# Second network's first product by Strassen's seven products instead of eight

## The chip, the cores and the metric

One Trainium2 chip, one core, one launch. The metric is the device time of that core in microseconds (us), the median over runs. TensorE (PE) multiplies, ScalarE (ACT) and VectorE (DVE) do the elementwise work, GpSimd (POOL) is nearly unused, and every DMA is issued from SyncE's queue (SP).

## The reference

Softmax-normalised linear attention (4 batches, 8 heads, 576 positions, width 64) gives x of 2304 tokens by 512. Two networks follow, each with a first product 512 to 2048, an elementwise function and a second product 2048 to 512:

```python
x = _moe_ref(x=x, **moe_kwargs)        # h = x @ w_in; g = h * sigmoid(1.702 h); g @ w_out
return _moe2_ref(x=x, **moe2_kwargs)   # h = x @ w_in; g = h * tanh(softplus(h)); g @ w_out
```

The weights arrive as float64, and the kernel decodes them to float32 on the chip.

## The kernel before, in words

Tokens go in 6 blocks of NB = 384, the 2048 hidden features in 16 chunks of 128. Every float32 operand of the two networks is kept as a high and a low part (`F32R`), and each product is the sum of three matmuls: high by high, high by low, low by high (`SPLIT`).

**First network.** Step n of 96 is block n // 16, chunk n % 16. `gemm_in` (line 771) makes 4 x 3 matmuls of 384 columns into one of two PSUM banks h0, h1; `gelu` is a tanh on ACT (L784) and a product on DVE (L789); `gelu_split` copies the high part (ACT L339 or DVE) and subtracts for the low part (DVE L331); `gemm_out` of step n - 2 (L812) makes 4 x 3 matmuls into banks acc0 to acc3. The attention of the next block is mixed into these steps, on banks at0 and at1. At a block's end `x2_evac` reads acc twice, once on ACT (L837) and once on DVE (L844), and writes x2 as high and low part; four of the six blocks go to the DRAM tile `x2d` (384 KB per piece).

**Second network.** It runs over 48 pairs of chunks (6 blocks x 8 pairs). `gemm_in2` calls `gemm_in` for two chunks: 24 matmuls of 384 columns into a pair of banks hp. `mish` is one ACT operation over 768 elements (L920), a high copy and a low subtraction (L339, L331). `gemm_out2` of pair n - 2 makes 18 matmuls of 512 columns (L945) that accumulate over the 8 pairs into three of the four acc banks. `out_evac` (L965, L966) copies them out after the eighth pair. All weights of the second network are decoded once by `weight` and then stay in SBUF in the tiles W0 to W15; a chunk's w_in part is split into high and low there like everything else. `weight` is one 512 KB load and then L348 twice, L388, L395, L400, L339 and L331, each over 512 elements (L400 over 1024 halves).

**Order.** Nothing is issued as it is written. `Plan.op` collects every operation with the engines that it may run on, its cost and the keys that it reads and writes; `Plan.order` lists them by urgency over some forward and backward passes, and `emit` issues them in that order. So the order on PE, ACT, DVE, POOL and in SP's queue is fixed before the run. PE's order inside the two networks is held by one key, `spine`. In SP's queue a DMA that waits holds up those behind it.

Of the kernel before, what the change touches and what calls it, by code (L numbers as in the profile page):

```python
# [201 lines left out]
def pool_ns(n):  # L202
    return {512: 1256.0, 384: 972.0, 768: 1800.0}[n]
# [7 lines left out]
def tile_attention_moe_moe(  # L211
# [54 lines left out]
    x2d = dram.tile([NBLK - 2, P, NCC, 2, NB], F32, name="x2d")  # L266
# [3 lines left out]
    hctx, atctx = ExitStack(), ExitStack()  # L270
    hpool = hctx.enter_context(tc.tile_pool(name="h", bufs=1, space=bass.MemoryType.PSUM))
    hps = [hpool.tile([P, 512], F32, name=f"h{i}") for i in range(2)]
    atpool = atctx.enter_context(tc.tile_pool(name="at", bufs=1, space=bass.MemoryType.PSUM, side="right"))
    at = [atpool.tile([P, 512], F32, name=f"at{i}") for i in range(2)]
    hp2 = [None, None]
# [92 lines left out]
    def weight(m, io, fc):  # L368
        i = n_w[0]
        n_w[0] += 1  # L370
        r, a = raw[i % NRAW], dec[i % ND]
        rl, rh, da = ("raw", i % NRAW, 0), ("raw", i % NRAW, 1), ("dec", i % ND)
# [5 lines left out]
        else:  # L378
            dst = r
            src = w_ap[m][1][fc * P : (fc + 1) * P, :]  # L380
        dma(P * 4096, [], [rl, rh], lambda: dst, lambda: src)
# [18 lines left out]
        dve(512, [rl], [da], lambda: nc.vector.tensor_tensor(out=a, in0=a, in1=lo_w, op=ALU.add), pair=True)  # L400
        late = [("late",)] if fc >= NFC - NLATE else []
        copy(512, lambda: W[fc][:, io, 0:512], lambda: f32(a), [da] + late, [("W", io, fc, 0)])
        either(
            512,
            ALU.subtract,
            lambda: W[fc][:, io, 512:1024],
            lambda: f32(a),
            lambda: f32(W[fc][:, io, 0:512]),
            [da, ("W", io, fc, 0)],
            [("W", io, fc, 1)],  # L410
        )

# [393 lines left out]
    def gemm_out(n):  # L806
        fc = n % NFC
        for dm in range(NCC):
# [17 lines left out]

    def x2_evac(blk):
        buf = blk % 2
        x = xt[buf]
        for dm in range(NCC):  # L830
            a = acc[dm][:, 0:NB]
            keys = x_keys(buf, dm)
            act(
                NB,
                [("acc", dm)],
                keys[:2],
                lambda dm=dm, a=a: nc.scalar.activation(out=x[:, dm, 0, :], in_=a, func=AF.Copy, scale=0.5),  # L837
                psum=True,
            )
            dve(  # L840
                NB,
                [("acc", dm)] + keys[:2],
                keys[2:],
                lambda dm=dm, a=a: nc.vector.scalar_tensor_tensor(  # L844
                    out=x[:, dm, 1, :], in0=a, scalar=0.5, in1=f32(x[:, dm, 0, :]), op0=ALU.mult, op1=ALU.subtract
                ),
            )
            if blk < NBLK - 2:
                dma(P * 3072, keys, [("x2d", blk, dm)], lambda dm=dm: x2d[blk, :, dm], lambda dm=dm: f32(x[:, dm]))


    NGP = 3
    NTB = 3
    tb = []
    ob = [f32(t) for t in dec]
    blocks = [NBLK - 2, NBLK - 1] + list(range(NBLK - 2))
    NPR = NFC // 2
    NSB = NBLK * NPR
    LAG = 2

    def pool_first():
        sctx.close()
        late = ctx.enter_context(tc.tile_pool(name="late", bufs=1, side="right", reuse_waits="tile"))
        W.extend(late.tile([P, 2, 1024], F32R, name=f"W{i}") for i in range(NFC - NLATE, NFC))

    def pool_second():
        actx.close()
        bp = ctx.enter_context(tc.tile_pool(name="second", bufs=1, reuse_waits="tile"))
        g2.append(bp.tile([P, 2, 2, NB], F32R, name="g2_2"))
        tb.extend(bp.tile([P, 2, NB], F32, name=f"tb{i}") for i in range(NTB - 1))  # L870
        tb.append(gt2)

    def tb_keys(i):

        return [("tb", i)] + ([("gt", 0), ("gt", 1)] if i == NTB - 1 else [])

    def hb(n):
        i = (n + 1) % 2
        if hp2[i] is None:
            old = (hctx, atctx)[i]  # L880
            old.close()
            new = ctx.enter_context(
                tc.tile_pool(name=f"pair{i}", bufs=1, space=bass.MemoryType.PSUM, side=("left", "right")[i], reuse_waits="tile")
            )
            hp2[i] = new.tile([P, 2, 512], F32, name=f"hp{i}")
        return hp2[i][:, :, 0:NB]

    def hb_keys(n):
        return [("h", 0), ("h", 1)] if n % 2 else [("at", 0), ("at", 1)]

    def gemm_in2(n):
        bi, pr = divmod(n, NPR)
        for j in range(2):
            gemm_in(lambda j=j: hb(n)[:, j, :], [hb_keys(n)[j]] if j else hb_keys(n), bi % 2, 2 * pr + j)
        if pr == NPR - 1 and bi + 2 < NBLK:
            keys = [key for dm in range(NCC) for key in x_keys(bi % 2, dm)]
            dma(
                P * 12288,
                [("x2d", blocks[bi + 2], dm) for dm in range(NCC)],
                keys,  # L900
                lambda: f32(xt[bi % 2]),
                lambda: x2d[blocks[bi + 2]],
            )

    def mish(n):
        i = n % NTB
        tk = tb_keys(i)
        gi = (n + 1) % NGP
        gk = [("gg", gi, a) for a in range(2)]
        if gi == 0:  # L910
            gk = [[("gg", 0, a), ("g", 0, a), ("g", 1, a)] for a in range(2)]
        elif gi == 1:
            gk = [[("gg", 1, a), ("qT", 0, a), ("qT", 1, a)] for a in range(2)]
        else:
            gk = [[("gg", 2, a)] for a in range(2)]

        def fn():
            if n == 0:
                nc.scalar.preload_act_table_set("mish")
            nc.scalar.activation(out=tb[i], in_=hb(n), func=AF.Mish)  # L920

        act(768 + 1540 * (n == 0), hb_keys(n) + [("second",)], tk + ([("tables",)] if n == 0 else []), fn, psum=True)
        copy(768, lambda: g2[gi][:, :, 0, :], lambda: tb[i], tk, gk[0])
        either(
            768,
            ALU.subtract,
            lambda: g2[gi][:, :, 1, :],
            lambda: tb[i],
            lambda: f32(g2[gi][:, :, 0, :]),
            tk + gk[0][:1],  # L930
# [3 lines left out]
    def gemm_out2(n):  # L934
        bi, pr = divmod(n, NPR)
        gi = (n + 1) % NGP
        last = n == NSB - 1
        jc = [(j, c) for j in range(2) for c in range(NCT)]

        for j, c in sorted(jc, key=lambda x: x[::-1]) if last else jc:  # L940
            bank = (bi * NCT + c) % 4

            def mm(j=j, c=c, bank=bank):
                for i, (a, b) in enumerate(SPLIT):
                    nc.tensor.matmul(  # L945
                        out=acc[bank],
                        lhsT=g2[gi][:, j, a, c * P : (c + 1) * P],
# [5 lines left out]
            wk = [("W", 1, 2 * pr + j, a) for a in range(2)]  # L953
            pe(3 * mm_ns(512), wk + [("gg", gi, 0), ("gg", gi, 1)], [spine, ("acc", bank)], mm)

    def out_evac(bi):
        blk = blocks[bi]
        dst = out[blk * NB : (blk + 1) * NB, :].rearrange("(p c) e -> p c e", c=NCT)
        cuts = [(0, 512)] if bi < NBLK - 1 else [(0, 256), (256, 512)]
        for c in range(NCT):  # L960
            for k, (lo, hi) in enumerate(cuts):
                a = acc[(bi * NCT + c) % 4][:, lo:hi]
                o = ob[c][:, lo:hi]
                ways = [
                    (DVE, dve_ns(hi - lo), lambda a=a, o=o: nc.vector.tensor_copy(out=o, in_=a), False),  # L965
                    (ACT, act_ns(hi - lo, True), lambda a=a, o=o: nc.scalar.activation(out=o, in_=a, func=AF.Copy), False),  # L966
                ]
                keys = [("dec", c), ("ob", c, 1)] if len(cuts) == 1 else [("dec", c) if k == 0 else ("ob", c, 1)]
                plan.op(ways if len(cuts) == 1 else ways[k : k + 1], [("acc", (bi * NCT + c) % 4)], keys)
                dma(P * (hi - lo) * 4, keys, [], lambda c=c, lo=lo, hi=hi: dst[:, c, lo:hi], lambda o=o: o)  # L970

# [11 lines left out]
    FIRST_W = 24  # L983
# [12 lines left out]
    second = w_order(6)  # L996
# [5 lines left out]
    for n in range(NS):  # L1002
# [7 lines left out]
        if n >= 2:  # L1010
            gemm_out(n - 2)
            if fc == 1:
                x2_evac(t - 1)
        gelu_split(n)
        if fc == 2 and t < NBLK - 1:
# [16 lines left out]
    n_second = 0  # L1032

    def weights_to(top):
        nonlocal n_second
        while n_second < min(top, len(second)):
            weight(1, *second[n_second])
            n_second += 1

    for n in range(NSB + LAG):  # L1040
        if n < NSB:
            weights_to(FIRST_W + 4 * n)
            gemm_in2(n)
            mish(n)
# [41 lines left out]
```

## Time and profile before

| | us |
|---|---|
| median of 3 runs (887.15 to 888.34) | 887.47 |
| the profiled execution | 887.29 |
| its span, first to last instruction | 885.5 |
| PE busy in the span | 873.7 (99%) |
| DVE busy | 392.9 (44%) |
| ACT busy | 364.5 (41%) |
| data moved | 65.81 MB, mean 74 GB/s |
| granted TensorE clock | 1.000 (2.4 GHz) |

The profiled execution takes 1.8 us more than its span. Busy shares are averages over stages; "idle before" in a row of a group is the engine's idle time just ahead of these instructions, with what ended it.

### The profile page before, as it was taken

The numbers are of one execution on the slowest core, as the hardware profiler recorded it, in microseconds if no ns is written. First come the engines' busy times: TensorE is split into PE (matmuls) and PEld (weight loads), VectorE is DVE, ScalarE is ACT, GpSimd is POOL, SyncE is SP. The second block draws the span as 40 slices with busy tenths as digits, with TensorE's granted clock in tenths as the row PEclk, the third lists the DMA queues.
The fourth block names the chain that finished last, engine by engine and source line by source line (L and its number), as shares of the span: only waits on it lengthen the run. The fifth ranks groups of instructions, "written<-read, shape, count | busy, mean of one in ns | idle before, by whom it ended". The sixth has DMA issues, their size and how long they took to land.

```text
span 885.5 us, 12334 instructions
## 1 busy us (share of the span) xinstructions
PE 873.7 (99%) x4970; PEld 811.0 (92%) x4970; DVE 392.9 (44%) x764; ACT 364.5 (41%) x691; POOL 3.0 (0%) x19
## 2 busy tenths in 40 slices
PE   8999999999999999999999999999999999999998
PEld 5787899999999999999999999899899899899897
DVE  7999993272385376226999810110110111111111
ACT  6989863242353244224688721321321321321321
POOL 1000000000000000000000000000000000000000
PEclk9999999999999999999999999999999999999999
DMA  9775762011142032000356201002001101100001
GB/s 258 207 215 165 225 211 65 12 57 40 29 105 84 1 84 91 1 5 23 128 174 190 96 1 72 36 1 72 36 0 72 36 1 72 37 1 1 36 1 36
DMA packets 63145, 65.81 MB, mean 74 GB/s; under 512 B 32496, under 2 KB 54512, under 8 KB 62576
## 3 DMA queue, kind: packets, MB, share of 16 engines
q1 hardware_dynamic: 63088, 65.02, 24.1%
q8 instruction: 39, 0.64, 0.3%
q14 instruction: 18, 0.15, 0.1%
HBM read 54.00 MB, written 11.01 MB: 73 GB/s over the span
## 4 chain that ended last, share of the span: by engine, by line
PE 90%; DVE 4%; DMA 2%; ACT 2%; issue 1%; SPq 0%; DVEq 0%; ACTq 0%
PE hp L771 23%; PE acc L945 22%; PE acc L812 21%; PE h L771 20%; PE at L535 1%; DMA kt<-in_k_dram 1%; DVE dec L400 1%; PE at L654 1%; DVE dec L395 1%; PE at L683 1%; DMA raw<-in_moe_w_in_dram 1%; PE at L496 1%; PE at L692 1%; PE at L499 1%; DVE W L331 1%
## 5 line engine op out<-in xcount | busy, mean ns | idle before, releaser
L771 PE MATMUL h<-xt,W 128*128 128x384 f32 x1152 | 226.6, 340 | 2.4 <-DVE gt L789 0.7
L812 PE MATMUL acc<-g,W 128*128 128x384 f32 x1152 | 224.1, 339 | 1.9 <-DVE W L331 1.8
L771 PE MATMUL hp<-xt,W 128*128 128x384 f32 x1152 | 208.4, 335 | 0.0
L771 PEld LDWEIGHTS h<-xt,W 128*128 128x128 f32 x1152 | 200.5, 188 | 8.5 <-DVE xt L646 1.4
L945 PE MATMUL acc<-W,g 128*128 128x512 f32 x864 | 206.1, 392 | 0.0
L771 PEld LDWEIGHTS hp<-xt,W 128*128 128x128 f32 x1152 | 201.9, 188 | 3.7
L812 PEld LDWEIGHTS acc<-g,W 128*128 128x128 f32 x1152 | 200.3, 188 | 5.2 <-DVE W L331 2.7
L945 PEld LDWEIGHTS acc<-W,g 128*128 128x128 f32 x864 | 161.6, 188 | 32.7
L331 DVE TENSOR_TENSOR g<-gt,g 128x384 fp32r<-128x384 f32 (+1 forms) x112 | 68.6, 613 | 177.6 <-ACT g L339 177.5
L331 DVE TENSOR_TENSOR g<-tb,g 128x768 fp32r<-128x768 f32 x32 | 30.7, 958 | 212.7 <-ACT g L339 212.7
L920 ACT ACTIVATE tb<-hp 128x768 f32<-128x768 f32 x32 | 26.0, 813 | 178.7 <-PE hp L771 178.7
L339 ACT ACTIVATE g<-gt 128x384 fp32r<-128x384 f32 (+1 forms) x111 | 63.3, 570 | 76.4 <-PE acc L812 71.1
L784 ACT ACTIVATE gt<-h 128x384 f32<-128x384 f32 x96 | 47.0, 490 | 93.8 <-PE h L771 93.0
L789 DVE SCALAR_TENSOR_TENSOR gt<-gt,h 128x384 f32<-128x384 f32 x96 | 52.9, 551 | 66.2 <-ACT gt L784 66.1
L920 ACT ACTIVATE gt<-hp 128x768 f32<-128x768 f32 x16 | 13.0, 812 | 96.3 <-PE hp L771 96.3
L348 ACT ACTIVATE dec<-raw 128x512 f32<-128x512 f32 x63 | 42.1, 672 | 7.0 <-DVE W L331 5.2
L331 DVE TENSOR_TENSOR W<-dec,W 128x512 fp32r<-128x512 f32 x64 | 43.8, 687 | 1.7 <-ACT W L339 1.6
L400 DVE CUSTOM_DVE_ANT_0 dec<-raw,dec 128x1024 uint16<-128x1024 uint16 x64 | 43.9, 687 | 0.5
L395 DVE SCALAR_TENSOR_TENSOR dec<-raw,dec 128x512 int32<-128x512 int32 x64 | 43.9, 687 | 0.2
L348 ACT ACTIVATE raw<-raw 128x512 int32<-128x512 uint32 x62 | 41.6, 676 | 3.7 <-DMA raw<-in_moe_w_in_dram 2.3
L339 ACT ACTIVATE W<-dec 128x512 fp32r<-128x512 f32 x61 | 38.1, 628 | 3.8 <-DVE dec L400 3.5
L339 ACT ACTIVATE g<-tb 128x768 fp32r<-128x768 f32 x32 | 27.1, 846 | 1.0
(84 smaller groups left out, 386.8 us busy)
## 6 DMA issues: line engine op xcount, KB each, us to landing
raw<-in_moe_w_in_dram SPq DMA_DIRECT2D x32, 512.0 KB, 4.4
raw<-in_moe_w_out_dram SPq DMA_DIRECT2D x32, 512.0 KB, 3.9
x2d<-xt SPq DMA_DIRECT2D x16, 384.0 KB, 2.9
xt<-x2d SPq DMA_DIRECT2D x4, 1536.0 KB, 6.5
kt<-in_k_dram SPq DMA_DIRECT2D x16, 288.0 KB, 3.9
out_dram<-dec SPq DMA_DIRECT2D x15, 256.0 KB, 2.5
vt<-in_v_dram SPq DMA_DIRECT2D x24, 144.0 KB, 3.4
qt<-in_q_dram SPq DMA_DIRECT2D x24, 96.0 KB, 2.8
```

Of the source, the lines that this page charges most:

```text
L331: return lambda: engine.tensor_tensor(out=out(), in0=in0(), in1=in1(), op=op)
L339: (ACT, act_ns(n), lambda: nc.scalar.activation(out=out(), in_=in_(), func=AF.Copy), False),
L348: (ACT, act_ns(512), lambda: nc.scalar.activation(out=out, in_=in_, func=AF.Copy, scale=scale), False),
L395: lambda: nc.vector.scalar_tensor_tensor(out=a, in0=hi_w, scalar=-0x80000000, in1=a, op0=ALU.bitwise_and, op1=ALU.bitwise_or),
L400: dve(512, [rl], [da], lambda: nc.vector.tensor_tensor(out=a, in0=a, in1=lo_w, op=ALU.add), pair=True)
L496: nc.tensor.matmul(out=o, lhsT=ident[0:KP, 0:KP], rhs=t[:, j].rearrange("p c d -> p (c d)"), start=True, stop=False)
L771: nc.tensor.matmul(out=h(), lhsT=w_mm(fc, 0, a, cc), rhs=xt[buf][:, cc, b, :], start=cc == 0 and i == 0, stop=cc == NCC - 1 and i == 2,)
L784: act(NB, [hk, ("tables",)], [tk], lambda: nc.scalar.activation(out=t, in_=h, func=AF.Tanh, scale=0.851), psum=True)
L789: lambda: nc.vector.scalar_tensor_tensor(out=t, in0=t, scalar=1.0, in1=h, op0=ALU.add, op1=ALU.mult),
L812: nc.tensor.matmul(out=acc[dm][:, 0:NB], lhsT=w_mm(fc, 1, a, dm), rhs=g[n % 2][:, b, :], start=fc == 0 and i == 0, stop=fc == NFC - 1 and ...
L920: nc.scalar.activation(out=tb[i], in_=hb(n), func=AF.Mish)
L945: nc.tensor.matmul(out=acc[bank], lhsT=g2[gi][:, j, a, c * P : (c + 1) * P], rhs=w_mm(2 * pr + j, 1, b, 0, 512), start=pr == 0 and j == 0 ...
```

## The change

Two blocks of 384 tokens are taken together (768 tokens, NSB = 3 of them). For a pair of chunks the first product of the second network is seen as a 2 x 2 by 2 x 2 block product: w_in in four quarters of 256 x 128, x2 in four quarters of 256 x 384. Instead of eight block products, each with 2 x 3 matmuls, seven are made (`product`), of sums and differences of the quarters.

- **Weights.** `combine`, eight times during steps 24 to 80 of the first network, decodes two chunks of w_in, forms the sums and differences, splits all seven into high and low parts and writes them to the DRAM tile `combos` (1792 KB for each pair). In the second network `ring_load` brings them back four loads a pair into two sets of places in W8 to W15 (halves of W14 and W15 for the smallest). w_out still stays in SBUF; its 16 decodes come in the last block of the first network.
- **x2.** `x2_evac` reads acc once, writes plain float32 and sends all six blocks to `x2d` (192 KB per piece). `x_load` brings 768 tokens back into W0 to W3, `x_sums` makes the differences, `x_split` the high and low parts of the seven operands, in xt, W4 to W7 and one new tile.
- **After each product** (`after`): one copy out of PSUM and seven additions or subtractions of 384 elements per pair on DVE (two for product 4), which give four quarters of h; each then has its own mish, high copy and low subtraction over 384 elements (`activated`).
- **PSUM.** The products alternate between at0 and at1; the second product uses acc0 to acc3, h0 and h1 for the six groups of 128 tokens.
- **PE's order.** Product 0 of pair n, the sixth output group of pair n - 2, products 1 and 2, then an output group of pair n - 1 after each of products 2 to 6.

```diff
-    x2d = dram.tile([NBLK - 2, P, NCC, 2, NB], F32, name="x2d")
+    x2d = dram.tile([NBLK, P, NCC, NB], F32, name="x2d")
+    combos = dram.tile([NFC // 2, P, 3584], F32, name="combos")
...
+    def combine(j, n):
+        plan.op([(NONE, 0.0, lambda: None, False)], [("h", n % 2)], [("pace", j)])
+        ins, outs = 2 * (j % 2), 2 * (1 - j % 2)
+        (a0, d0), (a1, d1) = [decoded(1, 0, 2 * j + k, ins + k, k, [("pace", j)]) for k in range(2)]
...
+        either(256, ALU.add, s1, lambda: a21, lambda: a22, [d1, ("late",)], [ks[0]])
+        either(256, ALU.subtract, s2, s1, lambda: a11, [ks[0], d0], [ks[1]])
+        either(256, ALU.subtract, s4, lambda: a12, s2, [ks[1], d0, ("late",)], [ks[2]])
+        either(256, ALU.subtract, lambda: a21, lambda: a11, lambda: a21, [d0], [d1])
...
+            split(n, lambda t=t, n=n: t[:, 0:n], lambda t=t, n=n: t[:, n : 2 * n], src, keys, hk, lk)
+            dma(
+                P * n * 8,
+                hk + lk,
+                [("combo", j, u)],
+                lambda u=u, n=n: combos[j][:, u * 1024 : u * 1024 + 2 * n],
+                lambda t=t, n=n: f32(t[:, 0 : 2 * n]),
+            )
...
+    def ring(n, u):
+        if u < 3:
+            fc = 8 + 3 * (n % 2) + u
+            return fc, 0, 512, w_keys(fc)
+        fc = NFC - 2 + n % 4 // 2
+        return fc, n % 2 * 512, 256, [("W", 0, fc, n % 2)]
...
+    def product(n, k):
+        u, q = PLACE[k]
+        fc, at_, half, wk = ring(n, u)
+        key = bank(n, k)
+
+        def mm():
+            for cc in range(2):
+                for i, (a, b) in enumerate(SPLIT):
...
+                        lhsT=W[fc][:, 0, w : w + P],
+                        rhs=operand(k, b)[:, cc, :],
...
+        def added(name, of, op=ALU.add):
+            t, tk, mine = temp()
+            s, _, sk = live[of]
+            in0, in1 = (lambda: ps, s) if op == ALU.add else (s, lambda: ps)
+            dve(NB, [key, sk], tk, lambda: nc.vector.tensor_tensor(out=t(), in0=in0(), in1=in1(), op=op))
...
+    for n in range(NP):
+        for kk in range(7):
+            product(n, kk)
+            after(n, kk)
...
+            if kk == 0 and n >= 2:
+                gemm_out2(n - 2, 5)
+            if kk >= 2 and n >= 1:
+                gemm_out2(n - 1, kk - 2)
+            if n < NP - 1 and n % NPR == NPR - 1:
+                x_split(kk, False)
+            for u in {2: (0,), 4: (2,), 5: (1,), 6: (3,)}.get(kk, ()):
+                ring_load(n + 2, u)
+        if n % NPR == 1 and n + NPR < NP:
+            x_load(n // NPR + 1)
+            x_sums()
```

What the change does to the order, at three places. First PE in the middle of the second network. Before, a pair of chunks (line 771 is `gemm_in`, line 945 `gemm_out2`; hp0 and hp1 are the two pairs of PSUM banks):

```order
L771 MATMUL hp0_4300<-xt0_78,W10_75 128x384 [waits Activation_49]
L771 MATMUL hp0_4300<-xt0_78,W10_75 128x384 x11
L771 MATMUL hp0_4300<-xt0_78,W11_76 128x384 x12
L945 MATMUL acc2_93<-W6_71,g2_2_3618 128x512 [waits Activation_49]
L945 MATMUL acc2_93<-W6_71,g2_2_3618 128x512
L945 MATMUL acc2_93<-W6_71,g2_2_3618 128x512 [waits DVE_49]
L945 MATMUL acc3_94<-W6_71,g2_2_3618 128x512 x3
L945 MATMUL acc0_91<-W6_71,g2_2_3618 128x512 x3
```

Now, products 1 to 5 of a pair (line 1042 is `product`, line 1120 `gemm_out2`):

```order
L1042 MATMUL at0_104<-xt0_78,W10_75 128x384 [waits DMAHW3_49,DVE_49]
L1042 MATMUL at0_104<-xt0_78,W10_75 128x384 x5
L1042 MATMUL at1_105<-W4_69,W8_73 128x384 [waits Activation_49]
...
L1120 MATMUL acc0_92<-W10_75,g2_0_80 128x512 x3
L1120 MATMUL acc0_92<-W11_76,g2_1_81 128x512 x3
L1042 MATMUL at0_104<-W6_71,W9_74 128x384 [waits DMAHW4_49,DVE_49]
...
L1120 MATMUL acc1_93<-W10_75,g2_0_80 128x512 x3
L1120 MATMUL acc1_93<-W11_76,g2_1_81 128x512 x3
L1042 MATMUL at1_105<-second0_3818,W10_75 128x384 [waits DVE_49]
L1042 MATMUL at1_105<-second0_3818,W10_75 128x384 x5
L1120 MATMUL acc2_94<-W10_75,g2_0_80 128x512 x3
```

The runs of one width went from 24 and 18 matmuls to 6 (12 once a pair), each product waits for the engine that emptied its bank, and four of seven also for a DMA of the ring.

Second, DVE where the second network begins. Lines 392, 397 and 351 decode w_out, line 330 is a low part or a difference, line 1090 an addition after a product, line 907 the copy of x2:

```order
L330 TENSOR_TENSOR W13_400<-dec0_87,W13_400 128x512 [waits PE_49,Activation_49]
L1090 TENSOR_TENSOR stage3_3821<-at1_105,stage2_405 128x384 [waits PE_49]
L397 ISA dec1_88<-raw0_83,dec1_88 128x1024 [waits DVE_49]
L330 TENSOR_TENSOR raw3_86<-W3_68,raw2_85 128x768 [waits DMAHW2_49]
L1090 TENSOR_TENSOR stage4_3822<-h0_99,stage2_405 128x384 [waits PE_49]
L351 TENSOR_SCALAR raw1_84<-raw1_84 128x512 [waits DMAHW3_49]
L907 TENSOR_SCALAR stage7_3825<-acc1_93 128x384 [waits PE_49]
L385 TENSOR_SCALAR dec2_89<-dec2_89 128x512 [waits Activation_49]
L1090 TENSOR_TENSOR stage5_3823<-h1_100,stage3_3821 128x384 [waits DVE_49,PE_49]
```

The additions that free a PSUM bank stand between decodes of w_out that are not due for several pairs.

Third, SP's queue in the middle of the second network, where before only three outputs and one load of x2 stood per block:

```order
L321 DMA W8_73<-combos_91 128x1024 [waits DMAHW0_49,PE_49]
L321 DMA W10_75<-combos_91 128x1024 [waits DMAHW1_49,PE_49]
L321 DMA W9_74<-combos_91 128x1024 [waits DMAHW2_49,PE_49]
L321 DMA W14_401<-combos_91 128x512 [waits DMAHW3_49,PE_49]
L321 DMA W11_76<-combos_91 128x1024 [waits DMAHW4_49,PE_49]
L321 DMA W13_400<-combos_91 128x1024 [waits DMAHW5_49,PE_49]
```

Each of the four loads of a pair waits for the products that read the place it fills.

## Rows read from the trace of the kernel before

**Rows 1.** The page: span, busy time of the engines, PE and its clock by slices.
```profile
span 885.5 us, 12334 instructions
PE 873.7 (99%) x4970; PEld 811.0 (92%) x4970; DVE 392.9 (44%) x764; ACT 364.5 (41%) x691; POOL 3.0 (0%) x19
...
PE   8999999999999999999999999999999999999998
...
PEclk9999999999999999999999999999999999999999
```

**Rows 2.** Busy time by stretch of the span: PE, PEld, DVE, ACT, POOL; clock, DMA share, GB/s.
```profile
0.00:110.00 110.00, 102.41 (x641) 83.54 (x641) 102.74 (x227) 91.59 (x216) 2.99 (x19) 1.00 0.75 213
110.00:310.00 200.00, 199.97 (x1242) 195.26 (x1241) 104.17 (x214) 78.19 (x156) 0.00 (x0) 1.00 0.23 68
310.00:345.00 35.00, 34.60 (x283) 32.81 (x282) 26.05 (x64) 16.33 (x37) 0.00 (x0) 1.00 0.28 66
345.00:420.00 75.00, 74.74 (x434) 74.24 (x433) 31.65 (x58) 25.96 (x53) 0.00 (x0) 1.00 0.08 27
420.00:478.50 58.50, 58.50 (x338) 58.50 (x338) 56.49 (x107) 44.97 (x85) 0.00 (x0) 1.00 0.51 157
478.50:882.00 403.50, 403.50 (x2041) 366.66 (x2039) 71.33 (x97) 107.10 (x145) 0.00 (x0) 1.00 0.10 37
882.00:885.50 3.50, 0.00 (x0) 0.00 (x0) 0.42 (x1) 0.38 (x1) 0.00 (x0) 1.00 0.42 141
```

**Rows 3.** The chain that ended last, in order of time: start, us, what.
```profile
151.33 2.08 PE h L771 x12
...
499.36 4.18 PE hp L771 x24
503.54 4.12 PE acc L945 x18
...
545.06 4.20 PE acc L945 x18
```

**Rows 4.** PE in order of time, four short windows: start, us to the last end, instructions.
```profile
499.19 1.40 PE L771 MATMUL hp<-xt,W 128*128 128x384 f32 x7
501.99 1.37 PE L771 MATMUL hp<-xt,W 128*128 128x384 f32 x7
503.38 1.78 PE L945 MATMUL acc<-W,g 128*128 128x512 f32 x7
505.92 1.75 PE L945 MATMUL acc<-W,g 128*128 128x512 f32 x7
```

**Rows 5.** Groups by line and shape, with the mean ns of one instruction.
```profile
L771 PE MATMUL hp<-xt,W 128*128 128x384 f32 x1152 | 208.4, 335 | 0.0
L945 PE MATMUL acc<-W,g 128*128 128x512 f32 x864 | 206.1, 392 | 0.0
...
L331 DVE TENSOR_TENSOR g<-gt,g 128x384 fp32r<-128x384 f32 x96 | 53.3, 555 | 67.2 <-ACT g L339 67.1
...
L339 ACT ACTIVATE g<-gt 128x384 fp32r<-128x384 f32 x95 | 49.8, 524 | 75.9 <-PE acc L812 71.1 <-DVE qt L331 1.6 <-DVE dec L400 1.5
L784 ACT ACTIVATE gt<-h 128x384 f32<-128x384 f32 x96 | 47.0, 490 | 93.8 <-PE h L771 93.0 <-DVE dec L395 0.3 <-PE at L483 0.3
L395 DVE SCALAR_TENSOR_TENSOR dec<-raw,dec 128x512 int32<-128x512 int32 x64 | 43.9, 687 | 0.2
L400 DVE CUSTOM_DVE_ANT_0 dec<-raw,dec 128x1024 uint16<-128x1024 uint16 x64 | 43.9, 687 | 0.5
...
L331 DVE TENSOR_TENSOR g<-tb,g 128x768 fp32r<-128x768 f32 x32 | 30.7, 958 | 212.7 <-ACT g L339 212.7
...
L388 DVE TENSOR_SCALAR dec<-dec 128x512 int32<-128x512 int32 x64 | 26.6, 422 | 1.0 <-ACT dec L348 1.0
...
L646 DVE TENSOR_TENSOR xt<-at,xt 128x384 fp32r<-128x384 f32 x16 | 8.7, 546 | 0.7 <-ACT xt L641 0.5
...
L965 DVE COPY dec<-acc 128x256 f32<-128x256 f32 x3 | 1.3, 425 | 9.4 <-ACT dec L966 9.4
```

**Rows 6.** DMA issues: count, KB each, median us from issue to landing.
```profile
raw<-in_moe_w_in_dram SPq DMA_DIRECT2D x32, 512.0 KB, 4.4
...
x2d<-xt SPq DMA_DIRECT2D x16, 384.0 KB, 2.9
```

More of the change, by code (lines that the diff above doesn't have):

```diff
@@ L804, in gelu_split, with gemm_out @@
         )
-    def gemm_out(n):
+    def gemm_out(n, dms=range(NCC)):
         fc = n % NFC
-        for dm in range(NCC):
+        for dm in dms:
             def mm(dm=dm):
@@ L825, in gemm_out @@
             )
[L827 to L854, printed above, removed]
+    NSB = NBLK // 2
+    NPR = NFC // 2
+    NP = NSB * NPR
     ob = [f32(t) for t in dec]
[L856 to L859, printed above, removed]
+    second = []
     def pool_first():
@@ L864, in pool_first @@
         W.extend(late.tile([P, 2, 1024], F32R, name=f"W{i}") for i in range(NFC - NLATE, NFC))
+        stage.extend(late.tile([P, NB], F32, name=f"stage{i}") for i in range(3))
     def pool_second():
@@ L888, in hb_keys @@
[L888 to L915, printed above, removed]
+        second.extend(bp.tile([P, 2, 2, NB], F32R, name=f"second{i}") for i in range(3))
@@ new lines, in x2_evac, with xf @@
+    def x2_evac(blk):
+        for dm in range(NCC):
+            if blk < NBLK - 1:
+                i = (blk * NCC + dm) % 3
+                t, keys = lambda i=i: stage[i], [("stage", i)]
+            else:
+                t, keys, _ = temp()
+            from_psum(NB, t, acc[dm][:, 0:NB], [("acc", dm), ("second" if blk == NBLK - 1 else "late",)], keys, scale=0.5)
+            dma(P * 1536, keys, [("x2d", blk, dm)], lambda dm=dm: x2d[blk, :, dm], t)
+    def xf(i):
+        return f32(W[i][:, 0, 0 : 2 * NB])
@@ L917, in fn, with g_tile, activated @@
+    def g_tile(n, j):
+        t = g2[j] if n % 2 else second[1 + j]
+        return t.rearrange("p i a n -> p i (a n)")
+    def activated(n, j, half, t, tk):
+        first = n == 0 and (j, half) == (0, 0)
         def fn():
-            if n == 0:
+            if first:
                 nc.scalar.preload_act_table_set("mish")
-            nc.scalar.activation(out=tb[i], in_=hb(n), func=AF.Mish)
-        act(768 + 1540 * (n == 0), hb_keys(n) + [("second",)], tk + ([("tables",)] if n == 0 else []), fn, psum=True)
@@ L923, in mish @@
[L923 to L930, printed above, removed]
+            nc.scalar.activation(out=t(), in_=t(), func=AF.Mish)
+        tables = [("tables",)]
+        act(NB + 1540 * first, tk + ([] if first else tables), tk + (tables if first else []), fn)
+        gk = [[("gg", n % 2, j, half, a)] for a in range(2)]
@@ L944, in mm, with gemm_out2 @@
+    live = {}
+    out_banks = [("acc", i) for i in range(4)] + [("h", i) for i in range(2)]
+    def gemm_out2(n, c):
+        pr = n % NPR
+        half = c // NCT
+        def mm():
+            for j in range(2):
                 for i, (a, b) in enumerate(SPLIT):
                     nc.tensor.matmul(
-                        out=acc[bank],
-                        lhsT=g2[gi][:, j, a, c * P : (c + 1) * P],
+                        out=bank_of(out_banks[c]),
+                        lhsT=g_tile(n, j)[:, a, c * P : (c + 1) * P],
@@ L951, in mm @@
                     )
[L953 to L957, printed above, removed]
-        dst = out[blk * NB : (blk + 1) * NB, :].rearrange("(p c) e -> p c e", c=NCT)
[L959 to L970, printed above, removed]
+        wk = [("W", 1, 2 * pr + j, a) for j in range(2) for a in range(2)]
@@ L1014, in tile_attention_moe_moe @@
         gelu_split(n)
+        if n >= 24 and n % 7 == 3 and n < 24 + 7 * NPR:
+            combine((n - 24) // 7, n)
+        if n == NS - NFC + 8:
+            x_load(0)
+            x_sums()
+            for kk in range(5):
+                x_split(kk, True)
+        if n >= NS - 4 and n < NS:
+            ring_load(0, n - NS + 4)
         if fc == 2 and t < NBLK - 1:
```

271 lines of the change are left out of this document (211 added, 60 removed).

## The prediction, made before the change had been run

> **What bounds the kernel now.** Start with the page: PE is busy 99% of the span and its clock row shows full speed, the 2.4 GHz level, in all 40 slices [rows 1]. A busy share is an average, so look next at the stretches [rows 2]. Before 110 us PE has gaps (102.4 of 110 us) while DVE is busy for 102.7: the start is held by softmax and weight decoding. From 110 us to 882 us PE idles only 0.7 us in all (0.03, 0.4 and 0.26 in the second, third and fourth stretch), and DVE and ACT have room, except from 420 to 478.5 us, where the second network's weights are decoded and DVE is busy 56.5 of 58.5 us without one gap on PE. The second network is the stretch from 478.5 to 882 us: PE 403.5 of 403.5, DVE 71, ACT 107, DMA share 0.10. What PE does there is what it costs, and the change takes matmuls out of just this stretch. Last, the pitch of the matmuls: the chain has 12 matmuls of 384 columns in 2.08 us, 173.3 ns each [rows 3]. A mean of 335 or 392 ns [rows 5] is not a pitch, because neighbours overlap.
>
> **One thing to see before the sum.** In the second network 384- and 512-column matmuls alternate, and the first ones after a switch are slower. Seven matmuls last six pitches and one duration. For 512 columns (392 ns) the first seven after a switch take 1.78 us and the last seven 1.75 [rows 4]: (1.78 - 0.39) / 6 = 231.7 ns against 226.7. For 384 columns it is 1.40 against 1.37 [rows 4], 177.8 against 172.8 (the chain's 173.3 within rounding), so some 0.03 us are lost at each switch. Before, a switch comes after 24 or 18 matmuls; now after 6.
>
> **The sum for PE.** Before, from 478.5 us on: 48 pairs of 4.18 and 4.12 to 4.20 us [rows 3] with two steps of `gemm_out` between them (24 matmuls, 4.2 us), together the 403.5 us [rows 2]. After:
> - products: 24 pairs x 7 x 6 = 1008 matmuls (1152 before) x 173.3 ns = 174.7 us;
> - switches into a product: six a pair in some 23 pairs x 0.03 = 4.1 us;
> - second product: the same 864 matmuls, now in groups of six, thus all at the pitch behind a switch: 864 x 231.7 ns = 200.2 us;
> - the two steps of `gemm_out`: 24 x 173.3 = 4.2 us.
>
> That is 383.2 us, 20.3 less than 403.5. The bounds: if nothing were lost at a switch, 174.7 + 864 x 226.7 ns + 4.2 = 374.8 (28.7 less); if all ran at the slowest pitches seen, 177.8 ns and 4.20 / 18 = 233.3 ns [rows 3, 4], 179.2 + 201.6 + 4.2 = 385.0 (18.5 less). I take the middle value, since six in a row is what the row of the first seven measures.
>
> The row gives a pitch of 173.3 ns for 384 columns, 13.3 more than 384 / 2.4. The Trainium skill ("TensorE: Matmul & The Clock Gate", section "Wait — 56ns, not 53.3ns?") states N / 2.4 GHz plus about 2.5 ns; by that the 144 matmuls taken out would be worth 144 x 162.5 = 23.4 us and not 25.0, and the 403.5 us themselves would come out near 374, which the trace contradicts.
>
> **What must stay hidden.** Per pair, now 15.8 us of PE (7.3 + 0.2 + 8.3):
> - DVE: seven additions out of PSUM at 0.55 (as L646) [rows 5] and four subtractions at 0.56 (L331) [rows 5]: 6.1 us. ACT: one copy at 0.49, four mish and four copies at 0.52 (L784, L339) [rows 5]: 4.7 us. In pairs 7 and 15 the seven `x_split` add some 8.9 us on DVE (six subtractions of 768 at 0.96 (L331) [rows 5], one difference of 768, four operations of 384): 15.0 us of 15.8, but each is due only a pair later, so it is 21 us in 31.6.
> - Banks: product k + 2 waits until product k's bank has been read. Between them lie another product (1.04) and an output group (1.39), 2.4 us; the read takes 0.55, after at most one other DVE operation of 0.96. Product 4, read twice, has two groups and a product, 3.8 us. Nothing is queued long behind a waiting addition, since DVE is under half full. Cost 0.
> - DMA: 1792 KB a pair in 15.8 us are 116 GB/s; from 420 to 478.5 us 157 GB/s ran beside PE without a gap [rows 2]. A place in the ring comes free after product 2 and is needed two pairs later, some 25 us, and a 512 KB load lands in 4.4 us [rows 6]. In SP's queue a load stands behind outputs and x2 loads that wait on ACT or DVE; these waits are for work of the same pair, so they eat part of the 25 us, not all.
> - First network: eight `combine`, each on DVE 2 x (0.42 + 0.69 + 0.69) decoding (L388, L395, L400), four of 256 elements at some 0.42 (L965) [rows 5], three subtractions of 512 at 0.69 and one of 256: 7.8 us over seven steps of at least 4.16 us. In the fullest stretch, 310 to 345 us, DVE goes from 26.1 to about 34 of 35 us if none of it overlaps [rows 2]; a stretch as full as that (420 to 478.5) cost PE nothing, so I add 0.5 us, bounds 0 to 3. Gone from there are the splits of `x2_evac` on DVE; its new wait, a fourth piece of x2 for the first one's store, is 2.9 us [rows 6] plus a copy of 0.49 against about 5 us until acc3 is written again. Cost 0.
> - Changeover: in pair 0 no output groups lie between products 4, 5, 6 and 0, 1, 2 of the next pair, so there a bank has 1.04 to 2.1 us to be read, with w_out decodes at 0.69 in DVE's queue. I take 0.5 us, bounds 0 to 3.
> - Ends of blocks: 0.5 us for both, bounds 0 to 4 (a queue of 0.96 us operations ahead of an addition, twice). Start: the order changes a little, the load on DVE does not; 0, bounds -1.5 to 1.5. Tail: last matmul to the end 3.5 us as before [rows 2]; 0.
>
> Sum: -20.3 + 0.5 + 0.5 + 0.5 = -18.8 us. Against the profiled execution's 887.3 that is **868.5 us**; the median of the runs is 0.2 us higher, which I neglect.
>
> **The rivals.**
> 1. *The pitch settles* (16%). If the loss at a switch comes from something else in the old order, the matmuls run at 173.3 and 226.7: 887.3 - 28.7 + 1.5 = 860.1. Against it: rows 4 show the loss at both kinds of switch; for it: 12 and 12 matmuls of one width, with waits between, show none [rows 3].
> 2. *Waits come back* (18%). The additions sit in DVE's order behind operations of 0.7 to 1 us, and two banks leave 2.4 us. If one product a pair comes 0.4 us late, 22 x 0.4 = 9 us: 877. For it: DVE near full in pairs 7 and 15 and in the first network's middle; against it: 6.1 of 15.8 us in most pairs.
> 3. *The ring is late, slower than before* (3%). One queue carries all loads, in order. Should a load be held until its slack is gone, one landing of 4.4 us would show per pair, 22 x 4.4 = 97 us, less the 18.8 gained: about 965. It decides where loads come more than 25 us after the place is free, and costs more than the gain from 0.85 us of lateness per pair on. Against it: 25 us of slack.
> 4. *The clock falls* (1%). Both networks alternate two banks already, at a granted clock of 1.000 throughout [rows 1, 2]. If short waits between products brought the 1.2 GHz level, products would take 2 x 174.7 us and the run about 1043. The Trainium skill ("TensorE: Matmul & The Clock Gate", section "A second HAM failure mode: psum-queue depth-cycling") tells of such a case; the trace so far does not bear it out.
>
> **How the numbers follow.** The forecast has 60%, with a range of its own from 864 to 874; 868.5 is its value. The range for 8 in 10 reaches over rival 1 and to rival 2's value: 860 to 877. A measurement of this kernel can tell 0.2%, 1.8 us, from no change. Faster takes in the forecast and rivals 1 and 2 (94%), slower rivals 3 and 4 (4%); 2% are left for stalls that happen to eat the gain. A change that does not do what it says is ruled out by the order: 42 matmuls a pair stand there, 48 before.
>
> **What would show it.** In the profile after: 1008 matmuls on the product's line and 864 on `gemm_out2`'s; PE busy without gaps in the last 380 us at clock 1.00; pairs of about 15.8 us; output groups of six in 1.39 us (1.36 would be rival 1); DVE some 6 and ACT some 5 us a pair, DMA near 116 GB/s. Idle on PE before the product's line with DVE as releaser would be rival 2, with DMA rival 3. The prediction is wrong if the last stretch is not 18 to 29 us shorter, or if the first network ends more than 3 us later than at 478.5 us.

## The result, and the profile after

The changed kernel takes **867.67 us** (867.02 to 869.05), the kernel before beside it 887.57 (887.15 to 888.34): a ratio of 0.9777, 95% interval 0.976 to 0.9794. The forecast was 868.5, its range 860 to 877. The profiled execution takes 867.2 us, 1.8 of it outside its span, as before.

The page of the changed kernel answers to [rows 1] and [rows 6]: span, busy time, PE and its clock by slices, all DMA, then four of the issues (count, KB each, median us to landing).

```profile
span 865.4 us, 12857 instructions
PE 850.7 (98%) x4826; PEld 786.0 (91%) x4826; DVE 529.0 (61%) x1053; ACT 412.5 (48%) x838; POOL 6.5 (1%) x21
...
PE   8899999999999999999999999999999999999998
...
PEclk9999999999999999999999999999999999999999
...
DMA packets 83742, 121.43 MB, mean 140 GB/s; under 512 B 34784, under 2 KB 59616, under 8 KB 83680
...
W<-combos SPq DMA_DIRECT2D x72, 512.0 KB, 3.6
...
combos<-raw SPq DMA_DIRECT2D x24, 512.0 KB, 2.7
W<-combos SPq DMA_DIRECT2D x24, 256.0 KB, 2.8
...
x2d<-stage SPq DMA_DIRECT2D x23, 192.0 KB, 2.0
```

PE has exactly 144 matmuls fewer, 4826 for 4970; DVE is busy for 136 us more, and 121 MB are moved instead of 66. PE stays the bound, and the clock stays at full speed as long as PE works (the 0.95 below is the tail behind its last matmul). In the windows of the changed kernel (columns as in [rows 2]) the fifth and sixth end where its second network begins and ends, and the last is one pair of chunks:

```profile
0.00:110.00 110.00, 101.46 (x641) 83.06 (x641) 103.05 (x227) 93.08 (x219) 2.97 (x19) 1.00 0.75 215
110.00:310.00 200.00, 198.68 (x1230) 193.62 (x1229) 125.84 (x258) 91.25 (x183) 3.54 (x2) 1.00 0.34 109
310.00:345.00 35.00, 34.39 (x281) 31.95 (x279) 29.17 (x73) 20.26 (x44) 0.00 (x0) 1.00 0.43 119
345.00:420.00 75.00, 74.40 (x431) 73.96 (x432) 47.46 (x93) 34.35 (x67) 0.00 (x0) 1.00 0.40 135
420.00:481.00 61.00, 61.00 (x353) 61.00 (x352) 54.26 (x100) 34.55 (x65) 0.00 (x0) 1.00 0.68 214
481.00:862.00 381.00, 380.79 (x1898) 342.42 (x1896) 168.80 (x306) 138.74 (x261) 0.00 (x0) 1.00 0.42 127
862.00:865.40 3.40, 0.00 (x0) 0.00 (x0) 0.42 (x1) 0.26 (x1) 0.00 (x0) 0.95 0.39 130
615.90:631.70 15.80, 15.80 (x80) 14.18 (x79) 6.04 (x12) 5.78 (x11) 0.00 (x0) 1.00 0.56 175
```

The second network runs from 481.1 to 861.8 us, without a gap on PE: 380.7 us, where from its first product (478.35) to its last matmul (882.0) it took 403.65. The first network ends 2.7 us later than before (481.1 for 478.35) and PE idles 1.3 us between 110 and 310 us, where it idled 0.03 [rows 2]. The chain of the changed kernel for one pair (start, us, what) shows the pitches:

```profile
601.16 1.07 PE at L1042 x6
602.23 1.40 PE h L1120 x6
603.62 2.09 PE at L1042 x12
605.71 1.40 PE acc L1120 x6
607.11 1.04 PE at L1042 x6
608.15 1.40 PE acc L1120 x6
609.55 1.04 PE at L1042 x6
610.59 1.40 PE acc L1120 x6
```

Six output matmuls take 1.40 us, as the row of the first seven after a switch promised [rows 4]. Over all pairs, from the starts of the matmuls in the trace, the pitch of the output matmuls is 231.4 ns and that of the product's 174.9.

The waits of PE from 110 to 481 us in the changed kernel (waiting work, what ended it, us in total, times, longest) have grown; line 687 is the low part of the attention's x for the next block:

```profile
PE h L812 <- DVE xt L687: 2.5, 4, 0.8
```

Over the same part of the kernel before, where line 646 is the same operation:

```profile
PE h L771 <- DVE xt L646: 0.4, 1, 0.4
PE at L654 <- DVE qt L331: 0.3, 1, 0.3
```

So the view that grew is not the second network's but the first's. PE of the changed kernel at the four places, each where a block of 384 tokens begins (start, us, instructions, in brackets the idle time before):

```profile
120.09 0.61 PE L812 MATMUL h<-xt,W 128*128 128x384 f32 x2 [0.44 <-DVE xt L687]
...
267.61 0.62 PE L812 MATMUL h<-xt,W 128*128 128x384 f32 x2 [0.82 <-DVE xt L687]
...
345.06 0.62 PE L812 MATMUL h<-xt,W 128*128 128x384 f32 x2 [0.66 <-DVE xt L687]
...
415.49 1.14 PE L812 MATMUL h<-xt,W 128*128 128x384 f32 x5 [0.54 <-DVE xt L687]
```

### The profile page after: what moved, and what is told of

It is laid out like the page before. It is cut to its first block, busy times and chain, and to the rows that moved or that the text cites. A ratio compares the mean times of both kernels' runs of the same rounds, so it can differ in the third digit from the quotient of the medians.

```text
span 865.4 us, 12857 instructions
## 1 busy us (share of the span) xinstructions
PE 850.7 (98%) x4826; PEld 786.0 (91%) x4826; DVE 529.0 (61%) x1053; ACT 412.5 (48%) x838; POOL 6.5 (1%) x21
## 4 chain that ended last, share of the span: by engine, by line
PE 83%; DVE 10%; ACT 4%; DMA 2%; issue 1%; SPq 0%; DVEq 0%; ACTq 0%
PE at L1042 20%; PE acc L853 19%; PE h L812 18%; PE acc L1120 15%; PE h L1120 8%; DVE dec L392 2%; DVE dec L397 2%; DMA raw<-in_moe_w_in_dram 1%; DVE W L330 1%; DVE g L330 1%; DVE dec L385 1%; DVE gt L830 1%; ACT raw L347 1%; ACT dec L347 1%; PE at L576 1%
## 5 line engine op out<-in xcount | busy, mean ns | idle before, releaser
L1042 PE MATMUL at<-xt,W 128*128 128x384 f32 x570 | 115.2, 337 | 0.0
L1042 PEld LDWEIGHTS at<-xt,W 128*128 128x128 f32 x570 | 102.3, 188 | 7.8
L330 DVE TENSOR_TENSOR g<-gt,g 128x384 fp32r<-128x384 f32 x111 | 61.6, 555 | 70.2 <-ACT g L338 69.7
L1090 DVE TENSOR_TENSOR stage<-at,stage 128x384 f32<-128x384 f32 x94 | 51.3, 556 | 72.3 <-PE at L1042 72.2
L338 ACT ACTIVATE g<-gt 128x384 fp32r<-128x384 f32 x111 | 58.2, 524 | 72.2 <-PE acc L853 67.0
L1120 PE MATMUL acc<-W,second 128*128 128x512 f32 x288 | 74.3, 393 | 0.0
L1120 PE MATMUL acc<-W,g 128*128 128x512 f32 x288 | 74.0, 394 | 0.0
L1120 PEld LDWEIGHTS acc<-W,g 128*128 128x128 f32 x288 | 53.4, 188 | 8.8
L1120 PEld LDWEIGHTS acc<-W,second 128*128 128x128 f32 x288 | 53.4, 188 | 8.4
L1042 PE MATMUL at<-W,W 128*128 128x384 f32 x276 | 55.5, 335 | 0.0
```

The costliest lines, as they stand in the source:

```text
L330: return lambda: engine.tensor_tensor(out=out(), in0=in0(), in1=in1(), op=op)
L338: (ACT, act_ns(n), lambda: nc.scalar.activation(out=out(), in_=in_(), func=AF.Copy), False),
L1042: nc.tensor.matmul(out=bank_of(key)[:, 0:NB], lhsT=W[fc][:, 0, w : w + P], rhs=operand(k, b)[:, cc, :], start=cc == 0 and i == 0, stop=cc ...
L1090: dve(NB, [key, sk], tk, lambda: nc.vector.tensor_tensor(out=t(), in0=in0(), in1=in1(), op=op))
L1120: nc.tensor.matmul(out=bank_of(out_banks[c]), lhsT=g_tile(n, j)[:, a, c * P : (c + 1) * P], rhs=w_mm(2 * pr + j, 1, b, 0, 512), start=pr = ...
```

## The experiments

**The theory** after the result: in the second network nothing but PE's own matmuls counts, at the pitch behind a switch; the 2 us by which the first network is later than forecast come from the operations of `combine`, which stand on DVE and ACT ahead of the attention's last operation for the next block. The rivals: the loss of pitch has another cause than the switch of width; banks, additions or the ring cost something hidden; the first network's loss comes from the DMA traffic of `combine`, or from GpSimd. The planner decides the whole order anew for each version, so a wait can come or go with the order and not with the work that was changed. The start also moves by a microsecond or two, with the order and from one execution to the next; so beside each time stands where the first product begins in the profiled execution (481.1 us in the changed kernel).

**The eighth product put back.** Product 6 is made twice into the same bank, 144 matmuls more, with everything else as changed.

```diff
-            for cc in range(2):
+            for cc in (0, 1) * (1 + (k == 6)):
...
-        pe(6 * mm_ns(NB), wk + [("xo", k, a, c) for a in range(2) for c in range(2)], [spine, key], mm)
+        pe((6 + 6 * (k == 6)) * mm_ns(NB), wk + [("xo", k, a, c) for a in range(2) for c in range(2)], [spine, key], mm)
```

> The seventh product is made twice, into the same place, so that eight products per pair run with everything else of the change left. Theory (TensorE's own work is the whole of the second network's time): 24 x 6 x 174.9 ns = 25.2 us more, 892.9, and the difference to the kernel before, some 5.4 us, is what the change costs apart from the saved product. Rival (part of the second network's time is waiting that a longer product would cover): less than 20 us more.

Measured: **893.33 us** (892.65 to 894.2), 25.7 more than the changed kernel; ratio to the kernel before 1.0057 (1.004 to 1.0075). The first product begins at 482.9 us. The window of its second network, with the last 1.9 us of the first:

```profile
481.00:889.00 408.00, 407.77 (x2052) 369.44 (x2050) 170.71 (x308) 140.06 (x263) 0.00 (x0) 1.00 0.39 119
```

No wait of PE's in it. From its first product to its last matmul the second network takes 405.9 us, 25.2 more than in the changed kernel, and 144 x 174.9 ns are 25.2; the 25.7 of the medians come from two sets of runs, in which the kernel before took 887.57 and 887.99. The gain is thus the matmuls taken out, and the rest of the change costs 893.3 - 888.0 = 5.3 us; 2.3 of it lie in the second network (405.9 for 403.65), where the matmuls have the slower pitches. By the rule that the prediction quoted from the Trainium skill ("TensorE: Matmul & The Clock Gate", section "Wait — 56ns, not 53.3ns?") they would be worth an estimated 23.4; the run decides for the rows' pitch.

**One set of places for the ring.** A pair's four pieces go to W8 to W11 always, and a load starts one pair ahead instead of two.

```diff
-        if u < 3:
-            fc = 8 + 3 * (n % 2) + u
-            return fc, 0, 512, w_keys(fc)
-        fc = NFC - 2 + n % 4 // 2
-        return fc, n % 2 * 512, 256, [("W", 0, fc, n % 2)]
+        fc = 8 + u
+        return fc, 0, 512 if u < 3 else 256, w_keys(fc)
...
-    for u in range(4):
-        ring_load(1, u)
...
-                ring_load(n + 2, u)
+                ring_load(n + 1, u)
```

> The ring holds one set of places and not two: a load waits for the product of the pair just before and is due 8 to 11 us later, not 25. Theory (a load lands in 3.6 us and nothing in the queue holds it long): no product waits, 867.7 within 1 us. Rival (queue or bandwidth leave little of the slack): products wait for the ring by some us per pair, 880 or more.

Measured: **868.27 us** (867.64 to 870.25), the same as with two sets. The profile shows no wait for a DMA; PE's only wait in the second network is this one, at its beginning:

```profile
PE at L1039 <- DVE second L330: 1.2, 1, 1.2
```

The profiled execution is the slowest of the four, 870.25 us: its first product begins at 483.2 us, and the 2 us are lost before 75 us already, with PE's order the same. Its second network takes 381.6 us, 0.9 more; the wait of 1.2 us is partly made up by the product's pitch, 174.0 ns in place of 174.9. No load is waited for: with half the slack the ring is still early, and rival 3 has nothing to stand on.

**Every addition made twice.** The second addition writes the same value again, so DVE has seven operations more per pair and a bank is read for twice as long.

```diff
-            dve(NB, [key, sk], tk, lambda: nc.vector.tensor_tensor(out=t(), in0=in0(), in1=in1(), op=op))
+            for _ in range(2):
+                dve(NB, [key, sk], tk, lambda: nc.vector.tensor_tensor(out=t(), in0=in0(), in1=in1(), op=op))
```

> Every addition after a product is made twice on VectorE, 7 x 0.55 = 3.9 us more per pair, so 10 of 15.7 us and each bank is held 0.5 us longer. Theory (two banks and 2.4 us between uses leave room): products wait nowhere but at the changeover and perhaps in pairs 7 and 15, 867.7 to 870. Rival (reading the banks is near its limit): waits of some tenths of a us at several products of each pair, 875 or more.

Measured: **870.11 us** (869.21 to 871.5), 2.4 more; ratio to before 0.98 (0.9782 to 0.9818); the first product begins at 481.6 us. One of its fullest pairs in a window (sums and splits of x2 for the next tokens are among it; a pair without them has some 9.5 us of DVE), then PE's waits of its second network:

```profile
600.00:615.80 15.80, 15.80 (x80) 14.18 (x79) 13.72 (x25) 7.53 (x15) 0.00 (x0) 1.00 0.65 203
```

```profile
PE at L1042 <- DVE gt L1091: 0.6, 1, 0.6
```

In this window DVE is busy 13.72 of 15.8 us, and PE still has no gap. The second network takes 382.2 us, 1.5 more, and these are lost in its first two pairs, where few output groups lie between the products: the place of the "changeover" term. Elsewhere the 2.4 us between a bank's products are enough, and rival 2's wait in every pair stays away even so.

**Two output groups together.** After products 0, 2 and 4 two groups follow, so a switch comes after 12 output matmuls and not 6.

```diff
+                gemm_out2(n - 2, 4)
                 gemm_out2(n - 2, 5)
...
-            if kk >= 2 and n >= 1:
+            if kk in (2, 4) and n >= 1:
                 gemm_out2(n - 1, kk - 2)
+                gemm_out2(n - 1, kk - 1)
```

> Output groups of the second network stand in pairs, after products 0, 2 and 4, so matmuls of one width come in runs of 12, with three switches each way per pair and not six. Theory (each switch of width costs some pitch, the more the shorter the run): output matmuls at about 230.0 ns (231.4 in the changed kernel), products at about 174.1 (174.9): 24 x (36 x 1.4 + 42 x 0.8) ns = 2.0 us less, 865.7. Rival (the time between a product and the next one on its bank decides): product 0 now has only one product of 1.04 us between it and the last use of its bank, and TensorE waits 0.1 to 0.3 us there in each pair, so 868 to 873.

Measured: **868.12 us** (867.86 to 868.89), the first product at 481.2: nothing gained. The output pitch falls as little as from 231.4 to 230.8 ns, the product's rises to 175.3, and waits for a bank come to 0.76 us in all, only at the beginning:

```profile
PE at L1042 <- DVE gt L1090: 0.5, 1, 0.5
```

Neither side had this: the per-pair waits of the rival do not show, and half as many switches do not bring the theory's 2 us. The starts of the matmuls, taken by their place in the group, show why: of twelve output matmuls the first eight average 231.7 ns and the last four 228.5. The groups of 18 before have the same shape, 231.5 in the first eight and 228.5 behind, 229.9 over all. The slow stretch behind a switch is longer than a group of six, and twelve barely leave it. The products lose more in return, since their first six behind twelve output matmuls average 176.1 ns. So the loss of pitch isn't a fixed price for each switch that one could save by halving their number.

**One width.** The output matmuls have 384 columns and not 512. This version leaves out the last 128 columns of the output, so its total says nothing; only the pitches count.

```diff
-                        out=bank_of(out_banks[c]),
+                        out=bank_of(out_banks[c])[:, 0:NB],
...
-                        rhs=w_mm(2 * pr + j, 1, b, 0, 512),
+                        rhs=w_mm(2 * pr + j, 1, b, 0, NB),
```

> Left out: the last 128 of the 512 output columns (copied from other columns), so the second network's second product runs with 384 columns like the first, everything else in its place; the output copies are cut in two. Theory (a switch of width is what costs pitch): products and output matmuls both run at 173.3 to 173.6 ns, 24 x 78 x 173.4 = 324.6 us plus 4.2 for the second network. Rival (the waits or the change of operand tiles at each group cost it): products stay near 174.9 and the output matmuls show some 2 to 5 ns over 173.3 too, 328 us or more.

Measured: products at 174.1 ns, output matmuls at 174.3 (one execution, 818.05 us). PE in order of time:

```profile
600.14 1.22 PE L1120 MATMUL h<-W,g 128*128 128x384 f32 x6
601.20 1.21 PE L1042 MATMUL at<-xt,W 128*128 128x384 f32 x6
```

With one width the two lines start 1.06 and 1.05 us apart. Against the chain's 173.3 ns [rows 3] the products lose 0.8 ns instead of 1.6; the output matmuls lose 1.0, where at 512 columns they lose 4.7 over 226.7. With one width no place in a group of six stands out, 173.7 to 174.7 ns. So most of the loss goes with mixing widths. The last 1 ns or so does not, and what that is stays open.

**Where the combinations stand.** Eight calls of `combine` come at steps 19, 23, 35, 39, 51, 55, 67 and 71 instead of every seventh step from 24; these leave the last steps of each block to the attention.

```diff
-        if n >= 24 and n % 7 == 3 and n < 24 + 7 * NPR:
-            combine((n - 24) // 7, n)
+        if n in PACE:
+            combine(PACE.index(n), n)
```

> The eight weight combinations start at steps 19, 23, 35, 39, 51, 55, 67 and 71 of the first network, in stretches without attention, not at 24, 31, 38 and so on. Theory (DVE work of a combination beside the attention of a block makes TensorE wait, about 2.1 us in all, on top of 0.6 us that the start is late): the first product comes at about 479.0 us of the span and not at 481.1, and the time is about 865.6. Rival (the added DMA traffic, or the copies of x2 with their store waits, makes the first network late): the first product stays near 481 and the time near 867.7.

Measured: **863.92 us** (863.67 to 865.49), ratio to before 0.973 (0.9712 to 0.9748): 3.75 less than the changed kernel (3.2 between the profiled executions), and the fastest version of all that leave nothing out. Its PE waits from 110 to 478 us, and three windows:

```profile
PE h L812 <- DVE xt L687: 0.3, 1, 0.3
```

```profile
310.00:345.00 35.00, 35.00 (x287) 33.31 (x286) 27.40 (x66) 16.55 (x37) 0.00 (x0) 1.00 0.36 100
345.00:420.00 75.00, 75.00 (x437) 74.87 (x436) 46.65 (x89) 37.65 (x73) 0.00 (x0) 1.00 0.43 138
478.00:859.00 381.00, 380.61 (x1897) 342.43 (x1896) 168.26 (x305) 139.02 (x261) 0.00 (x0) 1.00 0.42 126
```

DVE has 46.65 us of work from 345 to 420 us, against 47.46 in the changed kernel, and PE none of its waits: the amount is the same, the place is not. The first product begins at 478.0 us, even 0.3 before the kernel without combinations; the second network is unchanged.

What stood ahead of L687 at the four places of the changed kernel is only in part a combination. At 267 us it was; at 345 us it was too, but the kernel before waits 0.39 us at the same place. At 120 and 415 us it was not: the first combination begins on DVE at 157.28 us, and the last one ends at 395.7. What stands there is a subtraction of the attention itself, which in the kernel before came behind this operation, and a decode of w_out:

```profile
118.82 0.95 DVE L330 TENSOR_TENSOR qt<-qt,qs 128x768 f32<-128x768 f32 x1
119.69 0.35 DVE L687 TENSOR_TENSOR xt<-at,xt 128x192 fp32r<-128x192 f32 x1
...
414.28 0.69 DVE L397 CUSTOM_DVE_ANT_0 dec<-raw,dec 128x1024 uint16<-128x1024 uint16 x1
414.88 1.01 DVE L687 TENSOR_TENSOR xt<-at,xt 128x384 fp32r<-128x384 f32 x2
```

These two waits, 0.98 of the 2.46 us, come from the order that the planner made, and go with it. So moving the calls helps, but the theory has the cause of only about half of the waits; why the planner's order turned out so is open.

**No arithmetic in the combinations.** This version leaves out decoding, sums and splits of `combine`: as many bytes are loaded (of another input) and written as they are.

```diff
-        (a0, d0), (a1, d1) = [decoded(1, 0, 2 * j + k, ins + k, k, [("pace", j)]) for k in range(2)]
...
+        for k in range(2):
+            ri = ins + k
+            dma(
+                P * 4096,
+                [("pace", j)],
+                [("raw", ri, 0), ("raw", ri, 1)],
...
```

> Left out: the decoding, sums and splits of the weight combinations. The same number of bytes is loaded and written to the DRAM tile at the same steps, from another input, so the second network computes with wrong weights. Theory (work on VectorE and ScalarE beside the attention makes TensorE wait): the waits at 267, 345 and 415 us go, the first product comes at about 479 us of the span and not 481.1, time about 865.5. Rival (the DMA traffic or the queue delays the attention's loads): the first product stays at 481 and the time at 867.7.

Measured: **864.39 us** (864.14 to 865.37), 3.3 less, the first product at 478.6. From 110 to 310 us PE has no gap:

```profile
110.00:310.00 200.00, 200.00 (x1241) 195.35 (x1240) 93.69 (x191) 71.81 (x144) 0.00 (x0) 1.00 0.33 110
```

DVE is busy for 32 us less and ACT for 19, while the DMA moves 110 GB/s as in the changed kernel's 109. Three of the four waits are gone; the one near 343 us is left (0.6 us), and the kernel before has it too (0.39). So it is not the transfers. The wait at 120 us is gone too, though no combination stands near it: what this version took away is the arithmetic together with the order that the planner had made for it, and it can't tell the two apart.

**Nothing of it on GpSimd.** The planner had put two subtractions of `combine` on POOL. The changed kernel, in order of time (start, us):

```profile
265.24 0.42 DVE L330 TENSOR_TENSOR stage<-dec,dec 128x256 f32<-128x256 f32 x1
265.33 1.47 POOL L330 TENSOR_TENSOR raw<-dec,raw 128x512 fp32r<-128x512 f32 x1 [67.20 <-ACT raw L338]
...
265.57 1.51 DVE L330 TENSOR_TENSOR dec<-dec,dec 128x256 f32<-128x256 f32 x1
...
265.80 0.49 ACT L682 ACTIVATE xt<-at 128x384 fp32r<-128x384 f32 x1 [0.55 <-PE at L724]
...
267.01 0.55 DVE L687 TENSOR_TENSOR xt<-at,xt 128x384 fp32r<-128x384 f32 x1
```

The second DVE operation takes 1.51 us beside POOL's 1.47, though the first, of the same size, takes 0.42; it ends 0.28 us after POOL does, and L687, for which PE waits at 267.6, comes only then. Here a rule of the Trainium skill bears ("SBUF — State Buffer", section "Who interferes with whom"): the port pair that VectorE and GpSimd share is an exclusive lock, VectorE's second SBUF input comes through it, and the order of issue decides which of the two is blocked. The trace agrees: the stretched subtraction reads two inputs, starts 0.24 us after POOL's and ends 0.28 us after it. Does this make the wait? The version keeps these operations off POOL:

```diff
-        plan.op([(DVE, dve_ns(n), on(nc.vector), True), (POOL, pool_ns(n), on(nc.gpsimd), True)], reads, writes)
+        plan.op([(DVE, dve_ns(n), on(nc.vector), True)], reads, writes)
```

> The two subtractions of the weight combinations that the plan gave to GpSimd run on VectorE. In the changed kernel one of them (265.3 to 266.8 us) stands beside a VectorE subtraction of 256 elements that took 1.51 us where others take 0.41, and the operation after it is what TensorE waits 0.82 us for at 267.6 us. Theory (the two engines block each other, and this makes that wait): the wait goes, the 256-element subtraction takes 0.4 us, the waits at 120, 345 and 415 us (0.44, 0.66, 0.54) stay, and the time is 0.8 us less, 866.9. Rival (the wait is only VectorE's load): it stays, with a VectorE operation of 0.69 more ahead of it, 867.7 or more.

Measured: **866.28 us** (865.91 to 867.8), 1.4 less, the first product at 480.0. The subtraction is back at 0.41 us, but DVE ahead of L687 and PE at the same place read:

```profile
266.25 0.93 DVE L654 TENSOR_REDUCE qs<-qt 128x12 f32<-128x768 f32 x1
...
266.81 0.44 PE L812 MATMUL h<-xt,W 128*128 128x384 f32 x1 [0.92 <-ACT xt L682]
267.70 0.61 PE L812 MATMUL h<-xt,W 128*128 128x384 f32 x2 [0.46 <-DVE xt L687]
```

Now it waits for ACT's and then DVE's operation on x, 1.4 us together. The waits at 120 and 345 us are gone, the one at 415 stays (0.54). The block between the engines is real, but this version doesn't decide whether it made the wait: the forecast that the wait goes was wrong, yet the order is another one, with a reduction of 0.93 us ahead of L687 that came behind it before. From the changed kernel's own rows one can estimate it: ACT's part of x was done at 266.29 us, a subtraction of 0.42 would have left DVE free by then, and L687 began at 267.01, so the block made some 0.7 of the 0.82 us there.

## Why the prediction was right, step by step

| step | forecast, us | measured, us |
|---|---|---|
| products with their switches | 178.8 | 176.3 (1008 x 174.9 ns) |
| second product | 200.2 | 199.9 (864 x 231.4 ns) |
| changeover and ends of blocks | 1.0 | 0.1 |
| end of the first network | +0.5 (0 to 3) | +2.7 |
| profiled execution | 868.5 | 867.2 |

- **The bound** was right: the gain is read from PE alone. The second network is 22.9 us shorter; putting 144 matmuls back makes it 25.2 longer.
- **The switch** was right for the output matmuls, 231.4 ns for 231.7 forecast, and rival 1 (226.7) is out: a group of six takes 1.40 us. For the products the term of 4.1 us was too large: the 0.03 us at each switch came from two windows rounded to 0.01, and 1.6 ns x 6 = 0.01 us is what a switch into a product cost. The reason given, a loss at each switch, holds in this form: one width takes most of it away, and behind a switch some eight output matmuls are slow, so that six in a row never see 226.7. What makes them slow is not shown.
- **What had to stay hidden** did, with room: DVE 6.0 and ACT 5.8 us in one pair (6.1 and 4.7 forecast), 127 GB/s over the second network (116 forecast for the weights alone), and no wait with a ring of half the depth. With the additions doubled only the beginning shows. At two alternating banks PE had no gap and the clock stayed at 1.00 for 380 us: the short waits that rival 4 needs did not come, and the case that it quoted from the Trainium skill was not put to the test.
- **The step that was mis-sized** is the first network: "a stretch as full as that (420 to 478.5) cost PE nothing, so I add 0.5 us". The stretch it leans on is nearly without attention. At the start of a block PE waits for one operation of DVE, and a few more operations of 0.4 to 1 us ahead of it show at once: 2.5 us of waits for 0.7, however much room DVE has over the 200 us around. At two of the four places these are operations of a combination, at the other two the planner's new order of older work. The remaining 0.9 us is no wait at a block's start: some 0.2 is lost before the first of them and some 0.7 while PE is busy, its cause open. The upper bound of 3 held, barely.
- The forecast's closeness is part luck: the second network with its changeover came 3.6 us better (22.9 less for 19.3), the first network 2.2 worse.
- Two slips in the working change nothing in the sum. With a duration of 335 ns the two pitches for 384 columns come out at 177.5 and 172.5 ns. And the stretch that would come out "near 374" by the rule quoted from the Trainium skill leaves out the two steps of `gemm_out`; with them that estimate is 377.6, still far from 403.5.

## What to carry to other kernels

Where PE is busy without a gap and the clock holds, count matmuls at the pitch that they have in the new neighbourhood, not at their best: the forecast stood on 231.7 and not 226.7 ns, worth 4 us here. When side work is spread over a stage, look for the operations for which the bound engine waits at the ends of tiles, and keep the side work off the steps before them: moving eight calls gave 3.75 us, more than the mean busy shares would have let one hope for. Where a planner makes the order, look also at what it did to the work that was not changed: here two of four waits came from that.

## What the runs showed of the hardware, unexpected

- A GpSimd subtraction of 512 float32 elements per partition took 1.47 and 2.07 us where DVE needs 0.69, and stretched a DVE subtraction of 256 beside it from 0.42 to 1.51 us.
- Matmuls of 384 columns run at 174.9 ns among groups of 512 and at 174.1 among groups of 384; those of 512 columns average 231.4 ns in groups of six, 230.8 in groups of twelve and 229.9 in groups of 18, because the first eight or so behind a switch of width run at about 231.6 and the later ones at 228.5.
- 512 KB from a DRAM tile land in 3.6 us while 127 GB/s in all are moved, and half the ring suffices.
